# Reordering the end of a block: one tile's norm and transposes earlier, another tile's square later

## The chip, the cores and the metric

One core of one Trainium2 chip runs one launch. The metric is the device time of that launch in microseconds (us). The kernel before was first measured at a median of 326.28 us (326.25 to 327.42, 3 runs).

## The reference, cut to what matters

Linear attention with a cosine weighting, then an RMS norm and a gated feed-forward layer over its output. Only the part from the numerators on is touched by the change.

```python
    num = np.einsum('bhsf,bhfd->bhsd', q_p, kv)
    den = np.einsum('bhsf,bhf->bhs', q_p, z)[..., None] + 1e-06
    return (num / den).astype(np.float32)
    # ... x: 4608 tokens x 512
    rms = np.sqrt(np.mean(x * x, axis=-1, keepdims=True) + 1e-06)
    xn = x / rms * rms_g
    g = xn @ w_gate
    silu = g * (1.0 / (1.0 + np.exp(-g)))
    val = xn @ w_val
    return (silu * val @ w_out).astype(np.float32)
```

## The kernel before

The program order of each engine is fixed by hand. Block 0 is the feed-forward layer of batch 0 (512 tokens). While its last stage, the products with `w_out` ("out products"), runs on TensorE, the attention output of batch 1 is prepared in four tiles of 128 tokens. In this text SBUF is the memory that holds the tiles, PSUM the memory that holds results of TensorE, in banks; the "first out bank" is `banks0[2]`, the one that is copied out first. Each tile goes through the same chain, over all engines:

```python
nd_pe(1, j, psA)      # TensorE: numerators and denominators into PSUM
nd_post(1, j, psA)    # VectorE: rec (L465, L468), division xt = num * rec (L469)
x_sq(1, j)            # ScalarE: square with sum (L480), then an accumulator read;
                      # GpSimd: rs = mean square ^ -0.5, one column (L485, "the power")
x_norm(1, j)          # VectorE: xn = xt * rs * gain row gb, one instruction (L507, "the norm")
x_tr_pe(1, j, bank)   # TensorE: four 128x128 transposes of xn into PSUM (L532)
x_tr_evac(...)        # ScalarE or VectorE: copy of the transposes into xnT
gval_mm(1, n, ...)    # TensorE: gate and value matmuls of block 1, read xnT (L546)
```

The end of block 0 in the kernel before (`out_mm(0, j, n, bank)` is one out product, L566; `tr1` is transposes and a ScalarE copy; `out_store` copies a finished bank out and stores it):

```python
    for n in range(NNT - 2):
        # ... earlier steps cut
        if n == 9:
            tr1(0, psV[0][:, :])
            out_mm(0, 0, n, banks0[0])
        if n in nd_at:                      # n = 4, 6, 8, 9: tiles 0 to 3
            j = nd_at[n]
            nd_pe(1, j, psA)
            nd_post(1, j, psA)
            if n == 9:
                x_norm(1, 1)                # second tile, behind the fourth's division
            x_sq(1, j)
        for j in range(1 if n == 9 else 0, 4):
            out_mm(0, j, n, banks0[j])
    for j in (2, 3):
        for n in (NNT - 2, NNT - 1):
            out_mm(0, j, n, banks0[j])
    out_store(V, 0, 2, banks0[2])
    x_norm(1, 2)
    out_mm(0, 0, NNT - 2, banks0[0])
    tr1(1, psV[1][:, :])                    # second tile's transposes
    out_store(A, 0, 3, banks0[3])
    out_mm(0, 0, NNT - 1, banks0[0])
    # ... two more out products
    gval_mm(1, 0, 0, (0, 256))              # block 1 starts: tiles 0 and 1, step 0
    out_store(A, 0, 1, banks0[1])
    tr1(2, psA[:, 0, :])
    x_norm(1, 3)
    x_tr_pe(1, 3, psC[1][:, :])             # fourth tile's transposes
    x_tr_evac(V, 1, 3, psC[1][:, :])
    gval_mm(1, 1, 1, (0, 256), ((psG, wg),))   # "the gate step" in the text below
```

## Time and profile before

| | kernel before |
|---|---|
| median of the first 3 runs | 326.28 us |
| span of the profiled execution | 323.8 us |
| TensorE busy | 315.8 us, 98% |
| second tile's norm starts / its transposes start | 53.84 / 54.64 us |
| first matmul of block 1 | 55.71 us |
| fourth tile's transposes / gate step | 56.81 / 57.03 us |

TensorE is the bound, so only its waits matter. The prediction shows the lines for them. Two more lines also belong here, from the timelines of VectorE and GpSimd (start us, length us, engine, line, operation, tile written and read):

```profile
55.10 1.41 DVE L507 SCALAR_TENSOR_TENSOR xn<-xt,rs,gb 128x512 bf16<-128x512 f32 x2
```

```profile
54.84 0.55 POOL L485 TENSOR_TENSOR rs<-ms,mhalf 128x1 f32<-128x1 f32 x1 [1.07 <-ACT scr L480]
```

The first is the third and the fourth tile's norm, back to back. The second is the fourth tile's power on GpSimd. It started 0.26 us before the first of these norms and took its usual 0.55 us.

### The profile page before, as it was taken

To read this page: it belongs to the slowest core of one execution; us is meant where nothing else is said; L and a number is where in the kernel's file an instruction comes from. 1 tells how busy PE (TensorE), PEld (TensorE's weight loads), DVE (VectorE), ACT (ScalarE), POOL (GpSimd) and SP (SyncE) were. 2 spreads that over 40 slices of the span, in tenths; PEclk is the share of its full clock that TensorE was granted. 3 is DMA by queue.
4 is the path that set the end of the run, shared out by engine and by line. 5 is a ranking of instruction groups with operands and counts; after the bars stand their busy time and mean duration, and the time that the engine had idled before them with its cause. 6 is when DMAs were issued, how large, how long until landed. Compare 5 with 4: busy or idle time off the path is not lost.

```text
span 323.8 us, 6006 instructions
## 1 busy us (share of the span) xinstructions
PE 315.8 (98%) x2185; PEld 162.4 (50%) x2220; DVE 183.9 (57%) x392; ACT 172.6 (53%) x343; POOL 40.3 (12%) x87
## 2 busy tenths in 40 slices
PE   8899999999999999999999999999999999999995
PEld 3587465654445444544454445444544444444443
DVE  6975677877666765577257745772577133203410
ACT  6974775864765466546564466455644333223321
POOL 4660202101110120012001120120011000000000
PEclk9999999999999999999999999999999999999999
DMA  7999999999699885986596669766721400020014
GB/s 280 284 199 236 300 216 301 263 200 181 171 276 210 222 197 162 179 224 196 162 251 162 179 193 214 195 160 213 107 57 35 130 32 2 29 101 0 2 33 98
DMA packets 93600, 53.88 MB, mean 166 GB/s; under 512 B 58497, under 2 KB 88193, under 8 KB 93570
## 3 DMA queue, kind: packets, MB, share of 16 engines
q1 hardware_dynamic: 86528, 48.65, 60.0%
q0 software_dynamic: 6880, 4.72, 9.8%
q8 instruction: 17, 0.28, 0.4%
q10 hardware_dynamic: 162, 0.13, 0.2%
q14 instruction: 13, 0.11, 0.1%
HBM read 37.75 MB, written 9.44 MB: 146 GB/s over the span
## 4 chain that ended last, share of the span: by engine, by line
PE 93%; DVE 3%; DMA 1%; issue 1%; ACT 1%; DVEq 0%
PE psV L546 27%; PE psG L546 27%; PE psC L566 26%; PE psA L370 3%; PE psA L414 2%; DVE kpm L254 1%; PE psG L566 1%; PE psG L693 1%; DMA rk<-in_k_dram 1%; PE psV L693 1%; PE psO L693 1%; PE psV L321 1%; DVE qp L254 0%; PE psA L422 0%; PE psG L977 0%
## 5 line engine op out<-in xcount | busy, mean ns | idle before, releaser
L561 DVE TENSOR_TENSOR hT<-psV,sg 128x512 bf16<-128x512 f32 x102 | 70.4, 690 | 96.3 <-PE psV L546 72.3
L555 ACT ACTIVATE sg<-psG 128x512 f32<-128x512 f32 x102 | 60.7, 595 | 66.6 <-PE psG L546 65.4
L546 PE MATMUL psV<-xnT,wv 128*128 128x512 bf16 (+1 forms) x365 | 92.1, 374 | 0.4
L546 PE MATMUL psG<-xnT,wg 128*128 128x512 bf16 (+1 forms) x352 | 90.8, 374 | 0.7
L566 PE MATMUL psC<-wo,hT 128*128 128x512 bf16 x382 | 88.5, 379 | 0.7
L546 PEld LDWEIGHTS <-wv 128*128 128x128 bf16 x416 | 40.7, 98 | 47.3
L566 PEld LDWEIGHTS <-hT 128*128 128x128 bf16 x420 | 40.2, 98 | 46.6
L546 PEld LDWEIGHTS <-wg 128*128 128x128 bf16 x416 | 38.7, 98 | 40.5 <-issue 0.3
L485 POOL TENSOR_TENSOR rs<-ms,mhalf 128x1 f32<-128x1 f32 x36 | 19.8, 551 | 182.1 <-ACT scr L480 182.1
L337 ACT COPY osb<-psC 128x512 f32<-128x512 f32 (+1 forms) x33 | 19.1, 580 | 43.0 <-PE psC L566 42.3
L507 DVE SCALAR_TENSOR_TENSOR xn<-xt,rs,gb 128x512 bf16<-128x512 f32 x35 | 26.4, 758 | 16.6 <-POOL rs L485 16.5
L480 ACT ACTIVATE scr<-xt 128x513 bf16<-128x513 f32 x36 | 22.8, 635 | 23.3 <-DVE xt L469 23.2
L252 ACT ACTIVATE kpm<-rk,tab 128x512 bf16<-128x512 f32 (+2 forms) x50 | 26.8, 587 | 1.6 <-DMA rk<-in_k_dram 1.6
L469 DVE TENSOR_TENSOR xt<-psA,rec 128x512 f32<-128x512 f32 x35 | 24.2, 692 | 1.2
L252 ACT ACTIVATE qp<-rq,tab 128x512 bf16<-128x512 f32 (+1 forms) x37 | 23.7, 662 | 0.0
L254 DVE TENSOR_SCALAR kpm<-rk,tab 128x512 bf16<-128x512 f32 (+2 forms) x56 | 19.6, 403 | 2.1 <-DMA rk<-in_k_dram 2.1
L254 DVE TENSOR_SCALAR qp<-rq,tab 128x512 bf16<-128x512 f32 (+1 forms) x37 | 16.0, 448 | 0.0
L414 PEld LDWEIGHTS <-qpT 128*128 128x128 bf16 x248 | 11.6, 98 | 6.8 <-ACT qpT L337 0.2
L414 PE MATMUL psA<-kvzs,qpT 128*128 128x65 bf16 x248 | 12.8, 194 | 0.1
L546 PE MATMUL psG<-xnt_tail,wg 128*128 128x512 bf16 x48 | 12.3, 379 | 0.1
L546 PE MATMUL psV<-xnt_tail,wv 128*128 128x512 bf16 x47 | 12.1, 379 | 0.0
L370 PEld LDWEIGHTS <-kpm 128*128 128x128 bf16 x280 | 9.4, 97 | 1.9 <-ACT vvm L337 0.5
(100 smaller groups left out, 187.7 us busy)
## 6 DMA issues: line engine op xcount, KB each, us to landing
out_dram<-osb SPq DMA_DIRECT2D x28, 256.0 KB, 2.5
rk<-in_k_dram SPq DMA_DIRECT2D x21, 256.0 KB, 3.5
rq<-in_q_dram SPq DMA_DIRECT2D x20, 256.0 KB, 3.1
rv<-in_v_dram SPq DMA_DIRECT2D x16, 256.0 KB, 3.0
rq<-in_q_dram SPq DMA_DIRECT2D x2, 1024.0 KB, 9.2
rv<-in_v_dram SPq DMA_DIRECT2D x4, 512.0 KB, 8.3
out_dram<-osb SPq DMA_DIRECT2D x14, 128.0 KB, 2.4
wo<-in_moe_w_out_dram POOLq DMA_DIRECT2D x4, 384.0 KB, 7.3
```

The source lines that it names most:

```text
L252: nc.scalar.activation(out=out_ap, in_=in_ap, func=AF.Relu, scale=scale)
L254: eng.tensor_scalar(out=out_ap, in0=in_ap, scalar1=scale, scalar2=0.0, op0=ALU.mult, op1=ALU.max)
L370: nc.tensor.matmul(pst[:, h % 2, h // 2 * E : (h // 2 + 1) * E], lhsT=kp_of(b)[:, 8 * c + (h if c < 4 else h % 4), :], rhs=vv_of(b)[:, c, ...
L414: nc.tensor.matmul(o[:, g, i, :], lhsT=qpT[(b, 0)][:, h, j * P : (j + 1) * P], rhs=kvz_of(b, h), start=True, stop=True,)
L469: nc.vector.tensor_tensor(out=xt[:, 0:DM].rearrange("p (b h d) -> p b h d", b=2, d=D), in0=o[:, :, :, 0:D], in1=rec[:, :, :].unsqueeze(3). ...
L480: nc.scalar.activation(out=scr[:, :], in_=xt[:, 0 : DM + 1], func=AF.Square, scale=1.0 / math.sqrt(DM), accum_out=ms[:, :],)
L485: nc.gpsimd.tensor_tensor(out=rs[:, :], in0=ms[:, :], in1=mhalf[:, :], op=ALU.pow)
L507: nc.vector.scalar_tensor_tensor(out=xn[:, :], in0=x_of[(b, j)][:, 0:DM], scalar=rs_of[(b, j)][:, :], in1=gb[:, :], op0=ALU.mult, op1=ALU. ...
L546: nc.tensor.matmul(pst[bank][:, cols[0] : cols[1]], lhsT=w[:, t, n * P : (n + 1) * P], rhs=x[:, t, cols[0] : cols[1]], start=(t == 0), sto ...
L555: nc.scalar.activation(out=sg[:, :], in_=psG[bank][:, :], func=AF.Silu)
L561: nc.vector.tensor_tensor(out=hTs[blk][:, n, :], in0=psV[bank][:, :], in1=sg[:, :], op=ALU.mult)
L566: nc.tensor.matmul(bank, lhsT=hTs[blk][:, n, j * P : (j + 1) * P], rhs=wo[:, n, :], start=(n == 0), stop=(n == NNT - 1),)
```

## The change

The intent is to take away TensorE's wait for the second tile's norm. The norm moves ahead of the fourth tile's division, the transposes move ahead of the last eight out products, and the fourth tile's square goes behind the copy of those transposes.

```diff
         if n == 9:
+            x_norm(1, 1)
             tr1(0, psV[0][:, :])
             out_mm(0, 0, n, banks0[0])
         if n in nd_at:
             j = nd_at[n]
             nd_pe(1, j, psA)
             nd_post(1, j, psA)
-            if n == 9:
-                x_norm(1, 1)
-            x_sq(1, j)
+            if n < 9:
+                x_sq(1, j)
         for j in range(1 if n == 9 else 0, 4):
             out_mm(0, j, n, banks0[j])
+    tr1(1, psV[1][:, :])
+    x_sq(1, 3)
     for j in (2, 3):
         for n in (NNT - 2, NNT - 1):
             out_mm(0, j, n, banks0[j])
     out_store(V, 0, 2, banks0[2])
     x_norm(1, 2)
-    out_mm(0, 0, NNT - 2, banks0[0])
-    tr1(1, psV[1][:, :])
     out_store(A, 0, 3, banks0[3])
-    out_mm(0, 0, NNT - 1, banks0[0])
-    for n in (NNT - 2, NNT - 1):
-        out_mm(0, 1, n, banks0[1])
+    for j in (0, 1):
+        for n in (NNT - 2, NNT - 1):
+            out_mm(0, j, n, banks0[j])
```

## The prediction

> **What bounds the kernel now.** I read the page first: the busy shares, then the shares of the chain that ended last.
>
> ```profile
> PE 315.8 (98%) x2185; PEld 162.4 (50%) x2220; DVE 183.9 (57%) x392; ACT 172.6 (53%) x343; POOL 40.3 (12%) x87
> ...
> PE 93%; DVE 3%; DMA 1%; issue 1%; ACT 1%; DVEq 0%
> ```
>
> TensorE is busy in 98% of a 323.8 us span and makes up 93% of the chain. A change of order that removes no matmul can therefore win only where TensorE waits. The view of waits, asked for TensorE and for its weight loads from 46 us to the end, says where that is. From there on one pair of waits names another engine, and both belong to the same instruction (its weight load and its matmul); I left out the waits put down to issue:
>
> ```profile
> PE psV L532 <- DVE xn L507: 0.2, 1, 0.2
> ...
> PEld L532 <- DVE xn L507: 0.6, 1, 0.6
> ```
>
> L532 is a transpose on TensorE, L507 the norm on VectorE that writes what it transposes. The chain in order of time, 52 to 57 us, shows that place, the end of block 0, where batch 1 is normalised and transposed between the last out products of block 0:
>
> ```profile
> 52.44 0.33 PE psA L414 x8
> ...
> 52.80 0.18 DVE rec L465
> ...
> 53.00 0.21 DVE rec L468
> ...
> 53.23 0.69 DVE xt L469
> 53.93 0.67 DVE xn L507
> 54.60 0.04 issue
> 54.64 0.40 PE psV L532 x4
> 55.04 0.65 PE psC L566 x3
> 55.69 0.03 issue
> 55.71 0.60 PE psG L546 x4
> ```
>
> From 52.8 to 54.6 us the chain runs over VectorE, not TensorE: it divides the fourth tile's numerators (L465 to L469), only then norms the second tile (L507), and TensorE waits for that norm. The timeline of TensorE gives the lost time (start us, length, instruction):
>
> ```profile
> 52.81 1.46 PE L566 MATMUL psG<-wo,hT 128*128 128x512 bf16 x6
> 54.10 0.38 PE L566 MATMUL psC<-wo,hT 128*128 128x512 bf16 x1
> 54.64 0.40 PE L532 MATMUL psV<-ident,xn 128*128 128x128 bf16 x4 [0.16 <-DVE xn L507]
> 54.88 0.81 PE L566 MATMUL psC<-wo,hT 128*128 128x512 bf16 x3
> 55.71 0.60 PE L546 MATMUL psG<-xnT,wg 128*128 128x256 bf16 x4
> ```
>
> Six products start 52.81 to 54.10, so 0.215 us from start to start. The product at 54.10 should be followed at 54.32, but the transposes start at 54.64: **0.32 us lost**. Three products from 54.88 should let the next block's first matmul start at 54.88 + 3 x 0.215 = 55.53; it starts at 55.71: **another 0.18 us**. The timeline of ScalarE explains the second: its copy of the second tile's transposes starts at 55.08 and takes 0.59 us, to 55.67, and the matmul reads that copy. Both losses, 0.50 us, have one cause: the second tile's norm is late. The "[0.16" counts only from the modelled end of the matmul, so I use starts.
>
> **What the Trainium skill says.** "TensorE: Matmul & The Clock Gate", section "Part 2: What happens when you issue a matmul", puts back-to-back 512-column matmuls at about 216 ns; the trace agrees with 0.215 us, so I count in that stride and not in the 0.38 us of one record. The same section says that weight loads may be pulled ahead but matmuls stay in program order. The trace agrees: the out products behind the waiting transposes needed nothing from VectorE and still started only at 54.88. "VectorE: DVE Perf Modes", section "The DRAIN you can't avoid", says the next operation doesn't start until the pipe is empty. Here the norm after the 0.69 us division starts 0.61 us after its start (53.23 to 53.84), so the trace shows a small overlap and I use measured start-to-start distances. "PSUM — Partial Sum Buffer", section "Engine vs sequencer instructions", calls the ScalarE and VectorE queues strict FIFO, which is why moving one instruction in them delays what it is put ahead of.
>
> **The change part by part.** The order of the two builds differs in 30 listed lines on TensorE, 13 on VectorE and 8 on ScalarE; instruction counts are equal. Nothing is removed: four steps move.
>
> 1. Norm of the second tile ahead of the fourth's division. Its input is ready: GpSimd's power ran at 51.24 for 0.55 us, to 51.79. The third tile's division starts at 51.61, so the norm starts at 51.61 + 0.61 = 52.22, against 53.84, and ends after its 0.74 us at 52.96. A weight load followed the old norm by 0.06 us (54.58 to 54.64), so it can start at 53.02. Cost: the fourth tile's first operation starts at 52.22 + 0.66 = 52.88 (the same distance as from 53.84 to the next at 54.50), against 52.80; its division starts at about 53.31 and ends at 54.00 instead of 53.92. It is 0.08 us later because VectorE was waiting 0.49 us there anyway.
>
> 2. Transposes of the second tile ahead of the eight last out products. The last product of step 9 starts at 53.03 (the second of the six above), so the transposes' turn is at 53.24, and their weight loads would naturally go 0.22 us before, at 53.02. The norm is just in time. Four transposes take 0.22 us (51.84 to 52.06 in the first tile's). Eight products follow from 53.46 for 8 x 0.215 = 1.73 us, so the next block's first matmul has its turn at **55.19 instead of 55.71: 0.52 us gained**. Its inputs are ready: transposes end at 53.64, the ScalarE copy runs 53.68 to 54.27. Its bank must be copied out first: its last product ends near 54.06, the copy on VectorE runs from about 54.15 to 54.83. Neither holds it.
>
> 3. The fourth tile's square behind that copy. The ScalarE queue starts it 0.48 us after the copy, at 54.16, against 54.04. The accumulator read follows at 54.70 and ends at 54.89; GpSimd follows by 0.07 us, 54.96 to 55.51. So its scale is 0.12 us later than before (55.39).
>
> 4. The fourth tile's own transposes become the next limit. Before, its norm started at 55.77 behind the third's, and the scale had long been there. Now the third's norm starts near 54.75 and VectorE is free at 55.42, but the scale comes at 55.51; norms follow the power by 0.04 us (80.78 + 0.55 to 81.37 in a later block), so 55.55 to 56.29, weight load at 56.35. TensorE reaches these transposes after eight half-width matmuls (0.87 us, 55.71 to 56.58 before) and the third tile's transposes (0.22 us): 55.19 + 0.87 + 0.22 = 56.28. It waits **some 0.07 us**. The matmuls after them start, with 0.24 us from waiting transpose to next matmul (54.64 to 54.88), at 56.59. Before it was 57.03.
>
> The sum on the path: 0.52 - 0.08 = **0.44 us gained at 57 us**. Downstream the second half of the first step needs the fourth tile's copy, which before ended at 57.72 for a start at 57.90; both move together. After 57 us no wait of TensorE on another engine is listed, so all later work should shift by the same 0.44 us. That is 0.13% of the time: 326.28 - 0.44 = 325.84, which I round to 325.85.
>
> **Rivals.**
>
> (a) The later square takes the place of the wait removed. The fourth tile now depends on transposes, copy, square, read, power, norm in a row: a slip of the second tile's norm by 0.1 us passes to the fourth's transposes as 0.1 us. The weight load of the second tile has 0.00 us to spare at 53.02. With slips of 0.1 to 0.2 us only 0.25 to 0.35 us would be left: about 326.0. For it speaks that the margins are that thin; against it that most distances used are measured on the same instructions 2 us apart.
>
> (b) The full 0.50 to 0.55 us comes through, if the fourth tile's scale arrives earlier than I count: about 325.75. For it: the wait I add is 0.07 us, within the error of my sums.
>
> (c) A transfer sets the next stage and the gain is given back. The value load of batch 2 is late: GpSimd waits for it 5.15 us, until 60.54. Against it: VectorE's casts of that load run at 64.85 and 66.05 behind other work and TensorE's first use of it starts at 66.56, so 4 us stand between. If it were true the time would be unchanged, 326.3.
>
> (d) VectorE becomes the bound and the kernel gets slower, by the norm before the division. VectorE is full from 54 to 56 us (1.00 us busy in each slice of the windows view), so this is its tightest stretch. But it has the same operations and loses an idle 0.49 us; I see at most 0.1 us of loss, 326.4.
>
> **Range and chances.** The steps leave a gain between 0.2 and 0.55 us, so 325.7 to 326.1 by mechanism. The three runs before were 326.25, 326.28 and 327.42, so one run can lie 1.1 us off and the medians may move by a tenth or two; I widen to 325.4 to 326.4. Two per cent would be 6.5 us; the whole stretch touched is 5 us long and held 0.50 us of lost time, so faster by 2% is all but impossible, and slower needs a stall the check of the order doesn't show. Chances: 0.005 faster, 0.985 within, 0.01 slower.
>
> **What would show it right or wrong.** In the changed profile: the norm of the second tile near 52.2 us and its transposes near 53.24, the wait of TensorE on that norm gone or under 0.1 us (step 1 and 2); the next block's first matmul near 55.2 with no idle of 0.18 us before it; the fourth tile's square near 54.16 and its power ending near 55.5 (step 3); the fourth tile's transposes near 56.35 with a small new wait on L507 (step 4); everything after 57 us some 0.44 us earlier, and a span near 323.4. Wrong would be: transposes at 53.4 or later, a first matmul of the next block that still waits for a copy, or a gain at 57 us that is gone by 100 us, which would mean a wait that this trace doesn't show.

## The result, and the profile after

The changed kernel took 326.24 us (median of 6 runs, 325.59 to 327.06). The kernel before, in the same series and its first runs, took 326.77 us (6 runs, 326.25 to 327.78). The ratio is 0.9984 with a 95% interval of 0.996 to 1.0007: the same within 2%, and not distinguishable from no change. A ratio here is the mean time of one kernel's runs over the mean of the other's in the same rounds, so it isn't quite the ratio of the medians quoted.

The profiled execution after has a span of 325.3 us, longer than the 323.8 us of before; it was the slowest of its six (327.06 us). So the two pages must not be subtracted. The busy line and the shares of the chain from its page:

```profile
PE 315.7 (97%) x2185; PEld 162.1 (50%) x2220; DVE 184.0 (57%) x392; ACT 172.6 (53%) x343; POOL 40.6 (12%) x87
...
PE 90%; DMA 4%; ACT 1%; issue 1%; SPq 1%; DVE 1%; POOL 0%; DVEq 0%; POOLq 0%
```

Work is the same, but a transfer and a bit of GpSimd have come into the chain. To compare stages I count from a common origin in both traces: the start of the third tile's division on VectorE (L469), the last instruction ahead of the moved norm. It is at 51.61 us before and 52.04 us after; what lies ahead of it is untouched by the change.

The chain after, in order of time, where before it ran over the fourth tile's division:

```profile
53.84 0.24 PE psV L532 x4
54.07 0.02 issue
54.10 0.40 ACT xnT L337
54.50 0.08 issue
54.58 0.73 ACT scr L480 x2
55.31 0.07 issue
55.38 0.91 POOL rs L485
56.30 0.03 issue
56.32 0.76 DVE xn L507
57.08 0.05 issue
57.13 0.40 PE psC L532 x4
```

The second tile's transposes (L532 at 53.84) no longer wait. The chain now leaves TensorE behind them and runs through copy, square, power and norm of the fourth tile, to its transposes at 57.13. One entry stands out: the power takes 0.9 us. The timelines of VectorE and of GpSimd, the same lines as were shown of before:

```profile
55.14 0.74 DVE L507 SCALAR_TENSOR_TENSOR xn<-xt,rs,gb 128x512 bf16<-128x512 f32 x1
56.32 0.75 DVE L507 SCALAR_TENSOR_TENSOR xn<-xt,rs,gb 128x512 bf16<-128x512 f32 x1 [0.44 <-POOL rs L485]
```

```profile
55.38 0.90 POOL L485 TENSOR_TENSOR rs<-ms,mhalf 128x1 f32<-128x1 f32 x1 [1.19 <-ACT scr L480]
```

The power now starts 0.24 us after the third tile's norm has started, and ends 0.40 us after that norm has ended (55.88 to 56.28). VectorE then sat idle 0.44 us for it. The timeline of TensorE:

```profile
55.62 0.60 PE L546 MATMUL psG<-xnT,wg 128*128 128x256 bf16 x4
56.06 0.60 PE L546 MATMUL psV<-xnT,wv 128*128 128x256 bf16 x4
56.50 0.39 PE L532 MATMUL psA<-ident,xn 128*128 128x128 bf16 x4
57.13 0.40 PE L532 MATMUL psC<-ident,xn 128*128 128x128 bf16 x4 [0.24 <-DVE xn L507]
57.36 0.60 PE L546 MATMUL psG<-xnT,wg 128*128 128x256 bf16 x4
```

| us after the origin | before | predicted | after |
|---|---|---|---|
| second tile's norm starts | 2.23 | 0.61 | 0.61 |
| its transposes start | 3.03 | 1.63 | 1.63 |
| first matmul of block 1 | 4.10 | 3.58 | 3.58 |
| fourth tile's power starts | 3.23 | 3.35 | 3.34 |
| fourth tile's power ends | 3.78 | 3.90 | 4.24 |
| its transposes start | 5.20 | 4.74 | 5.09 |
| gate step | 5.42 | 4.98 | 5.32 |

The change gained 0.52 us at the first matmul of block 1, exactly as worked out, and gave 0.42 us of it back at the fourth tile's transposes. **0.10 us is left at the gate step, not 0.44.**

### The profile page after: what moved, and what is told of

The parts are those of the page before. It is cut to its first block, busy times and chain, and to the rows that moved or that the text cites. A ratio compares the mean times of both kernels' runs of the same rounds, so it can differ in the third digit from the quotient of the medians.

```text
span 325.3 us, 6006 instructions
## 1 busy us (share of the span) xinstructions
PE 315.7 (97%) x2185; PEld 162.1 (50%) x2220; DVE 184.0 (57%) x392; ACT 172.6 (53%) x343; POOL 40.6 (12%) x87
## 4 chain that ended last, share of the span: by engine, by line
PE 90%; DMA 4%; ACT 1%; issue 1%; SPq 1%; DVE 1%; POOL 0%; DVEq 0%; POOLq 0%
PE psV L546 26%; PE psC L566 26%; PE psG L546 25%; DMA rv<-in_v_dram 4%; PE psA L370 3%; PE psA L414 2%; PE psG L566 1%; PE psG L693 1%; PE psV L693 1%; PE psO L693 1%; PE psV L321 1%; PE psA L422 0%; ACT scr L480 0%; SPq L82 0%; PE psG L977 0%
## 5 line engine op out<-in xcount | busy, mean ns | idle before, releaser
L561 DVE TENSOR_TENSOR hT<-psV,sg 128x512 bf16<-128x512 f32 x102 | 70.3, 689 | 97.4 <-PE psV L546 72.8
L469 DVE TENSOR_TENSOR xt<-psA,rec 128x512 f32<-128x512 f32 x35 | 24.2, 691 | 1.2
```

What stands on the lines that cost most here:

```text
L469: nc.vector.tensor_tensor(out=xt[:, 0:DM].rearrange("p (b h d) -> p b h d", b=2, d=D), in0=o[:, :, :, 0:D], in1=rec[:, :, :].unsqueeze(3). ...
L561: nc.vector.tensor_tensor(out=hTs[blk][:, n, :], in0=psV[bank][:, :], in1=sg[:, :], op=ALU.mult)
```

## The experiments

Two theories. **P**: the power on GpSimd stands still while the third tile's norm, an instruction with two inputs in SBUF, runs on VectorE. The Trainium skill states such a rule, in "SBUF — State Buffer", section "Who interferes with whom": "A DVE instruction with two SBUF inputs contends with a GpSimd instruction that reads SBUF". **Q**: the square that was put behind a copy is what makes the fourth tile late. A third question came with the first runs: does what is gained at the gate step reach the end?

### The changed kernel again: after_again

No edit.

> The changed kernel once more. All times below are counted from the start of the third tile's division on VectorE (L469, the last before the moved norm), so that executions whose opening took longer can be compared. Theory P (the fourth tile's power on GpSimd stands still while the third tile's norm, which reads two tiles from SBUF, runs on VectorE): the power takes 0.90 us again, the fourth tile's transposes start 5.09 and the first matmul of the next gate step 5.32 us after the origin, 0.10 us earlier than in the kernel before (5.42); the whole time is then only 0.1 us below before, a ratio near 0.9997. Rival C (the 0.90 us was an accident of that one execution): the power takes 0.55, the two come at 4.72 and 4.95, and the ratio is near 0.9985.

Measured: the power took 0.90 us again, transposes at 5.09, gate step at 5.33. Time 325.97 us (6 runs, 325.47 to 326.57) against 325.83 us (11 runs); ratio 1.000 (0.9981 to 1.002). Theory P's numbers hold to 0.01 us and the long power is no accident. The times of the stage repeat far better than the whole time does.

### Third tile's norm out of the way: third_first

```diff
-    out_store(V, 0, 2, banks0[2])
     x_norm(1, 2)
+    out_store(V, 0, 2, banks0[2])
```

> The third tile's norm is put ahead of the copy of the first out bank on VectorE, so it ends some 0.3 us before the fourth tile's power starts. Theory P: the power takes 0.55 us, the fourth tile's norm starts 3.93 us after the origin, its transposes come at 4.75 and the next gate step at 4.97; the first matmul of the next block waits for the later bank copy and starts at 3.66 instead of 3.58. Rival Q (the moved square is late because it sits behind the copy in the ScalarE queue, and that alone delays the fourth tile): the power ends as late as before, the transposes stay at 5.09 and the gate step at 5.32, or later.

Measured, timeline of GpSimd and of VectorE (the norm that waited is the fourth tile's):

```profile
54.93 0.55 POOL L485 TENSOR_TENSOR rs<-ms,mhalf 128x1 f32<-128x1 f32 x1 [1.19 <-ACT scr L480]
```

```profile
55.51 0.75 DVE L507 SCALAR_TENSOR_TENSOR xn<-xt,rs,gb 128x512 bf16<-128x512 f32 x1 [0.28 <-POOL rs L485]
```

The power starts 3.34 us after the origin, as in the changed kernel, and takes 0.55 us. First matmul of block 1 at 3.70, fourth tile's transposes at 4.80, gate step at 5.03. Theory P was right in the mechanism and 0.06 us off, mostly because the later bank copy held TensorE a little longer (3.70 for 3.66). Q falls: the square is as late as in the changed kernel, and the gate step is 0.29 us earlier. Time 325.75 us (6 runs) against 325.83 us, ratio 1.000 (0.9979 to 1.0022): nothing of it shows in the whole time. This execution had a wait of 0.69 us near 70 us, to which I come back.

### One input moved to PSUM, result wrong on purpose: psum_gain

```diff
     out_store(V, 0, 2, banks0[2])
-    x_norm(1, 2)
+    xn = four.tile([P, DM], BF16, name="xn", tag="xn")
+    nc.vector.scalar_tensor_tensor(
+        out=xn[:, :].rearrange("p (a c) -> p a c", a=2),
+        in0=x_of[(1, 2)][:, 0:DM].rearrange("p (a c) -> p a c", a=2),
+        scalar=rs_of[(1, 2)][:, :],
+        in1=psA[:, 1:2, 0:256].to_broadcast([P, 2, 256]),
+        op0=ALU.mult, op1=ALU.mult,
+    )
+    xn_of[(1, 2)] = xn
```

> Wrong result on purpose: the third tile's norm takes its second tensor from a PSUM bank instead of the gain row in SBUF, in the same place, of the same length, so that it reads one tensor from SBUF only. Theory P: the power, though it still starts while that norm runs, takes 0.55 us, and the fourth tile's transposes come near 4.72 and the gate step near 4.95. Rival Q, or any rival in which the place in time and not the second SBUF input makes the power long: 0.90 us, 5.09 and 5.32 unchanged.

Measured, timeline of VectorE and of GpSimd:

```profile
54.98 0.73 DVE L934 SCALAR_TENSOR_TENSOR xn<-xt,rs,psA 128x512 bf16<-128x512 f32 x1
```

```profile
55.22 0.55 POOL L485 TENSOR_TENSOR rs<-ms,mhalf 128x1 f32<-128x1 f32 x1 [1.19 <-ACT scr L480]
```

This is the sharpest of the tests. The instruction is in the same place and of the same length, the power starts 0.24 us into it as in the changed kernel, and yet it takes 0.55 us. Transposes at 4.73, gate step at 4.97. The second SBUF input was taken away, so that input is what makes the power stand still. (The stand-in also reads the same 256 columns twice; a change of that access pattern alone was not run, but the instruction's length did not move by more than 0.01 us.)

### The same overlap made in the kernel before: before_third_first

The edit is that of third_first, applied to the kernel before.

> The kernel before, with the third tile's norm ahead of the first bank's copy, which puts that norm over the power, where in the kernel before they only touched. Theory P: the norm runs from 2.89 to 3.63, the power starts at 3.23 as before but takes 0.80 us (0.40 after the norm's end) instead of 0.55. Later bank copy: next block at 4.29 instead of 4.10, gate step near 5.62. Rival (the long power belongs to the changed kernel's place): 0.55 us.

Measured: the norm ran from 2.89 to 3.64, the power started at 3.23 and took 0.81 us, to 4.04, again 0.40 us after the norm's end. Block 1 started at 4.29, the gate step came at 5.62. The changed kernel isn't needed for the effect.

### First part alone: norm_alone

```diff
         if n == 9:
+            x_norm(1, 1)
             tr1(0, psV[0][:, :])
...
-            if n == 9:
-                x_norm(1, 1)
             x_sq(1, j)
```

> Only the first part of the change: the second tile's norm ahead of the fourth's division; its transposes and the square stay where they were. Counted from the third tile's division. Theory P (power and two-tile norm exclude each other): the transposes no longer wait and start at 2.71, the copy behind the square ends at 3.74, so the next block starts at 3.78; the first out bank is done earlier than in the full change, so the third tile's norm runs from 2.91 to 3.65, the power starts at 3.30 inside it and ends 0.40 us after it, at 4.05 (0.75 us long); fourth tile's transposes at 4.90, next gate step at 5.13, so this part alone gains 0.29 us on the kernel before, more than the full change's 0.10. Rival (the parts add up, and the full change is the better): next gate step later than 5.32.

Measured, group of the power over the whole kernel (shortest/median/longest in ns), of this kernel and then of the kernel before:

```profile
L485 POOL TENSOR_TENSOR rs<-ms,mhalf x36: 548/550/749, 16.5 to 255.7; 128x1 f32<-128x1 f32 x36
```

```profile
L485 POOL TENSOR_TENSOR rs<-ms,mhalf x36: 548/550/568, 15.4 to 254.1; 128x1 f32<-128x1 f32 x36
```

Of 36 powers one is long, the fourth tile's: from 3.31 to 4.06, behind a norm from 2.91 to 3.65. Transposes at 2.72 without a wait, block 1 at 3.78, fourth tile's transposes at 4.90, gate step at 5.13: every number of the expectation within 0.01 us. So the first part alone gains 0.29 us at the gate step, three times the whole change. The rest of the change takes 0.19 us of that away. It is the earlier transposes that do it, since square_first (next) has them without the later square and comes to the same 5.32: they let the first out bank finish later, so its copy starts at 2.49 instead of 2.31, with it the third tile's norm, and with it the end of the long power. One execution, 327.19 us with a late opening (origin at 52.76 us); its whole time says nothing.

### The square not later: square_first

```diff
-    tr1(1, psV[1][:, :])
     x_sq(1, 3)
+    tr1(1, psV[1][:, :])
```

> The full change without the later square: the fourth tile's square goes ahead of the second tile's transposes and copy again. Theory P: the square starts at 2.51 instead of 2.54, so nothing is won: the power still starts inside the third tile's norm (3.10 to 3.84) and ends at 4.24, the fourth tile's transposes start at 5.09, the gate step at 5.32; the copy comes behind the square and the next block's first matmul starts at 3.62 instead of 3.58. Rival Q (the square put behind the copy is what delays the fourth tile): power ending by 3.9, transposes at 4.75, gate step under 5.0.

Measured: power from 3.30 to 4.24 (0.94 us), fourth tile's transposes at 5.08, gate step at 5.32. Q falls a second time: starting the power 0.04 us earlier only makes it 0.04 us longer. I was wrong on one number: block 1 started at 3.75, not 3.62. I had forgotten that the accumulator read stands between square and copy, so the copy starts at 3.13. The later square does serve the first matmul of block 1, by 0.17 us; the wait at the fourth tile then hides that.

### Second part without the first: transposes_alone

```diff
         if n == 9:
-            x_norm(1, 1)
             tr1(0, psV[0][:, :])
...
             nd_post(1, j, psA)
+            if n == 9:
+                x_norm(1, 1)
```

(against the changed kernel)

> The second part without the first: transposes and square as in the changed kernel, the norm of the second tile behind the fourth's division as before. Matmuls stay in order, so TensorE stands until the norm ends: transposes at 3.03 with nothing before them, next block at 5.0, the power again inside the third tile's norm, fourth tile's transposes near 6.53 and gate step near 6.77: 1.35 us later than in the kernel before.

Measured, timeline of TensorE:

```profile
54.95 0.40 PE L532 MATMUL psV<-ident,xn 128*128 128x128 bf16 x4 [1.23 <-DVE xn L507]
```

Transposes at 3.03 after a wait of 1.23 us, block 1 at 4.99, gate step at 6.73: 1.31 us later than before (1.35 expected). The out products behind the transposes could have run and did not. The earlier transposes are only worth having with the earlier norm.

### A version without the overlap: third_first_value and third_value_again

On top of third_first, block 1 starts with its value half, because its gate bank is now the one copied out last.

```diff
-    gval_mm(1, 0, 0, (0, 256))
+    gval_mm(1, 0, 0, (0, 256), ((psV, wv), (psG, wg)))
```

> As the run before, and the next block's first step takes its value half before its gate half, because the value bank is free early and the gate bank is now the late one. Theory P: first matmul of the next block at 3.58 again, power 0.55 us, fourth tile's transposes at 4.72 and next gate step at 4.95, now bound by the chain of square, power and norm with TensorE waiting under 0.1 us. Rival Q: 5.09 and 5.32 as in the changed kernel. The whole time would be 0.45 us below the kernel before (ratio 0.9986) under P if nothing later takes it back; if the late value load of batch 3, near 97 us, sets the next stage, the whole time moves by less than the gate step does.

> The change with the third tile's norm and the value half first, once more, for the whole time: gate step at 4.97. If the 0.45 us of the stage reach the end in most executions, the ratio is 0.998 to 0.9995 and the fastest execution is some 0.4 us under the fastest of before; if the late value load of batch 3 takes it back, the fastest is still 0.4 us under but the medians are nearly equal.

Measured, both times: power 0.55 us, first matmul of block 1 at 3.59 and 3.58, transposes at 4.74 and 4.73, gate step at 4.97. So this order gains 0.45 us at the gate step, the size that I had predicted for the change itself. The whole time: 325.44 us (6 runs, 325.02 to 327.45) against 325.83 us, ratio 0.9995 (0.997 to 1.0021); the second time 326.19 us (325.48 to 327.41) against 326.34 us, ratio 0.9995 (0.9971 to 1.002). In the first series its fastest execution is 0.5 us under the fastest of before (325.02 to 325.55), in the second 0.1 us (325.48 to 325.58), while its slowest are as slow as those of before. So a fastest execution some 0.4 us under that of before was seen in one series of two.

### Before against itself: before_again

> The kernel before against itself: what a ratio of this kind shows where there is nothing to show. Ratio 1.000 within some 0.002; power 0.55 us long, gate step 5.42 us after the third tile's division. If the waits of TensorE near 97 us (none in the one profile of before) belong to late loads and not to the change, they may show up here too; if the earlier gate step causes them, this profile has none.

Measured: 326.56 us (6 runs, 325.87 to 327.99) against 326.34 us for the same kernel (11 runs), ratio 1.0014 (0.9986 to 1.0043); gate step at 5.41, no wait after it. A difference of the size predicted (0.0013) can't be read from six runs.

### Where the whole time scatters

A table of the profiled executions splits each span at the origin and at the gate step.

| execution | origin at | gate step after origin | gate step to the end | wait after the gate step |
|---|---|---|---|---|
| before | 51.61 | 5.42 | 266.8 | none |
| before_again | 52.18 | 5.41 | 266.8 | none |
| before_third_first | 52.02 | 5.62 | 266.8 | none |
| transposes_alone | 51.92 | 6.73 | 266.8 | none |
| after | 52.04 | 5.32 | 267.9 | near 91 and 97 us |
| after_again | 51.71 | 5.33 | 266.9 | none |
| square_first | 51.76 | 5.32 | 266.8 | none |
| norm_alone | 52.76 | 5.13 | 267.5 | near 70 and 97 us |
| third_first | 51.59 | 5.03 | 267.7 | near 70 us |
| third_first_value | 52.00 | 4.97 | 266.8 | none |
| third_value_again | 51.82 | 4.97 | 268.1 | near 70, 91 and 97 us |
| psum_gain | 51.88 | 4.97 | 267.2 | near 97 us |
| queue_relief | 52.07 | 4.97 | 266.8 | none |
| all_three | 51.79 | 4.97 | 268.3 | near 97 us (0.07 us near 91) |

The opening moves the origin by up to 1.2 us from execution to execution. Where TensorE meets no further wait, 266.8 or 266.9 us follow the gate step, whatever the kernel: then the gain of the stage reaches the end whole. In six executions up to 1.5 us were lost again. Timeline of TensorE in the execution of after, then in that of third_first:

```profile
98.41 0.19 PE L370 MATMUL psA<-vvt,kpm 128*128 128x65 bf16 x1 [0.55 <-POOL vvt L339]
```

```profile
69.94 0.42 PE L414 MATMUL psA<-kvzs,qpT 128*128 128x65 bf16 x8 [0.69 <-DMA qpT<-qp]
```

At 97 us TensorE waits for the cast of batch 3's values, which waits for their load; at 70 us for queries transposed by DMA. Near 91 us the first matmuls of block 2 start up to 0.4 us late, where the waits name a transfer. These transfers are issued from SyncE's queue, in order. In the profile of before the second load of value heads was issued at 89.12 us, in that of after at 91.15 us, though TensorE was only 0.33 us later at the gate step. None of the four executions with a gate step at 5.41 or later had such a wait, six of the ten with an earlier one had (in two of the ten the loads themselves were reordered, as told next). That an earlier TensorE runs into these transfers more often is plausible from that; with so few profiled executions, it isn't shown.

Two runs tried to take the waits away, on top of third_first_value. all_three loads the small last piece of batch 3's values ahead of its second half of heads:

```diff
-                at(b, 14, "post", load_heads, "v", nb, 4, 8)
                 at(b, 14, "post", load_last, "v", nb)
+                at(b, 14, "post", load_heads, "v", nb, 4, 8)
```

> The change, with the third tile's norm first, the value half first, and one thing more: in block 1 the last 64 tokens of batch 3's values are loaded ahead of its last four heads, because in slow executions TensorE waited near 97 us for the cast of just that piece. Theory: gate step at 4.97 as in the run without it; the cast of that piece on GpSimd is done over 1 us ahead of its use, TensorE waits nowhere near 97 us, and the whole time is 0.4 to 0.8 us below the kernel before (ratio 0.9975 to 0.999), with a smaller spread. Rival (the waits near 97 us come from elsewhere, from queue order or transposes by DMA): spread of 1 us or more as before, and a median no better than the run with two of the three, which was 0.4 us below the kernel before.

Measured: 326.46 us (6 runs, 325.15 to 327.33) against 326.63 us (11 runs), ratio 0.9987 (0.9959 to 1.0016). The view of TensorE's waits after 46 us:

```profile
PE psA L370 <- DVE vvm L339: 1.3, 1, 1.3
```

The small piece came in time and the second half of heads, now issued last (at 91.65 us), came 1.3 us late. The expectation failed: reordering the loads moved the wait from one piece to the other.

queue_relief takes a load out of the way instead: the last 64 tokens of batch 3's queries go in behind the values.

```diff
                 n = (0, None, 6)[i] + p if b == 1 else 5 * i + p
+                if (which, nb, p) == ("q", 3, 4):
+                    n = 15
```

> As the run beside it, and the load of the last 64 tokens of batch 3's queries leaves SyncE's queue in block 1 ahead of the value loads and goes in behind them. Theory (SyncE's serial queue sets the value load, so TensorE's waits near 97 us come from what stands in front of it): the last value load of heads is issued 0.5 to 1.3 us earlier relative to the matmuls, TensorE waits nowhere near 97 us, the stretch from the gate step to the end is 266.8 us, and the median is 0.4 us or more below the kernel before. Rival (bandwidth, not the queue, sets it): the load is issued earlier and lands no earlier, with the same scatter.

Measured: 325.53 us (6 runs, 325.20 to 326.72) against 326.34 us (11 runs), ratio 0.9976 (0.9956 to 0.9997), the only interval that lies below 1. third_value_again in the same rounds, without this edit, took 326.19 us. No matmul waits in its profile after the gate step (one weight load waits 0.2 us for transposed queries, which delays no matmul). The second load of heads was issued 32.5 us after the gate step, against 32.9 and 34.2 us in the two executions without the edit, so the issue is earlier, though by less than expected in the first comparison. It beats the kernel before as far as six runs can tell, and barely: one interval of eight that just misses 1 is weak evidence. It wasn't run beside the changed kernel. How much of its 0.8 us belongs to the queue and how much to the gate step stays open.

## Why the prediction was right or wrong

The time lay inside the stated range: 326.24 us, 325.85 predicted, range 325.4 to 326.4. That is not much to be proud of, because the scatter of the executions alone fills this range. By its steps:

**The place of the loss and its cause: right.** TensorE's wait for the second tile's norm is gone.

**Steps 1 and 2: right to 0.01 us.** Norm at 0.61, transposes at 1.63 with no wait, first matmul of block 1 at 3.58 us after the origin. The thin margin of 0.00 us at the weight load held.

**Step 3: right up to the power's start, wrong at its end.** The square stood behind the copy in ScalarE's queue, 0.48 us after its start (54.10 to 54.58), as counted. "GpSimd follows by 0.07 us, 54.96 to 55.51": the power started where I put it (3.34 for 3.35), but took 0.90 us, not the 0.55 us that I took from its earlier records. This term of the sum was mis-sized by 0.35 us. I had written that the third tile's norm would start "near 54.75", thus ahead of the power, in the same section, and didn't ask what the two do to each other. In the profile of before no power had started inside a norm, so all 36 durations there were between 548 and 568 ns: a duration from records holds only for what ran beside them.

That profile did show the effect on another pair, which was overlooked. Timelines of VectorE and of GpSimd in the kernel before, in a later block:

```profile
120.60 0.86 DVE L507 SCALAR_TENSOR_TENSOR xn<-xt,rs,gb 128x512 bf16<-128x512 f32 x1 [2.08 <-POOL rs L485]
```

```profile
120.97 0.75 POOL L339 CAST vvt<-rv 64x256 bf16<-64x256 f32 x1
```

This cast of values on GpSimd starts inside a norm and takes 0.75 us; casts that start inside a product with one SBUF input (L561) take 0.39 to 0.40 us. It happens four times in every one of the 14 profiles. The longest norm of the kernel before (0.86 us, for the usual 0.74) would have led there.

**Step 4: right in kind, wrong in size.** The fourth tile's transposes did become the next limit. "It waits some 0.07 us" became 0.41 us: they were due at 4.68 (the third tile's start at 4.46, and 0.22 us) and started at 5.09. The net gain of the stage was therefore 0.10 us and not 0.44.

**"All later work should shift by the same": right where no transfer comes late**, shown by the constant 266.8 us. In the profiled execution of after it was wrong by 1.1 us, lost near 91 and 97 us, around the value load of batch 3: the prediction's own sign of being wrong, a gain "that is gone by 100 us". In after_again nothing was lost. Rival (c) named a late transfer, but at the values of batch 2 near 60 us, which did no harm; the ones that hurt come later.

**Rivals (a), (b), (d).** (a) had the right chain (transposes, copy, square, read, power, norm in a row) but the wrong cause, a slip of the second tile's norm; square_first shows that the square's place isn't it. (b) did not happen. (d) did not happen: the next block started early.

**A reading of the skill.** The prediction sets the 0.61 us from start to start against "VectorE: DVE Perf Modes", section "The DRAIN you can't avoid", as if the two differed. That section adds that a next operation that isn't held back starts earlier, so the overlap of 0.08 us agrees with it; no sum rests on this.

**The difference in medians.** 0.53 us between the medians looks like the predicted 0.44 us, and isn't evidence for it: the stage gained 0.10 us, the second series of the same kernel showed 325.97 against 325.83 us, and the kernel before against itself 326.56 against 326.34 us. Over the four series the median of the kernel before lay between 325.83 and 326.77 us.

## What to carry to other kernels

Before moving a VectorE instruction with two SBUF inputs, look what GpSimd will start while it runs: here a one-column operation took 0.75 to 0.94 us instead of 0.55, and it hurts where it stands in a chain that TensorE waits for. Look for such a pair elsewhere in the profile first; here it was there, with other instructions. Take a duration from the trace only together with what ran beside it. When a change is worth less than the scatter of whole executions, measure the stage from a common origin in the traces; here that repeated to 0.01 us, while medians of six runs moved by 0.2 us with no change at all.

## What the Trainium skill lacked or had wrong

- "SBUF — State Buffer", section "Who interferes with whom": the rule on two SBUF inputs holds here (0.90 us for 0.55 us, and 0.55 us again with one input in PSUM). The section gives two slow-down factors (6.8 and 1.5) but not when a blocked operation ends. Elsewhere the page has a time for a DMA whose descriptors GpSimd writes (section "A bandwidth-pool intuition that's wrong (but worth ruling out)": the end of the VectorE operation and about 115 ns), none for a GpSimd computation. The runs show that a power blocked by a norm ended 0.40 or 0.41 us after the norm's end in six executions, wherever it had started, and a cast of 64x256 values 0.27 us after it (four times in the kernel before).
- The same section says that issue order decides who blocks, and of the two-port modes that the pair is held for the whole instruction. With GpSimd first, the runs show less than that. A power in the lead did no harm to VectorE: in the kernel before a norm started 0.26 us into it, and both kept their usual 0.74 and 0.55 us; a product with two SBUF inputs (L494) started 0.05 us into another, and took 0.41 us (0.42 us with no power beside it), the power 0.57 us. A cast in the lead did harm: a norm that started 0.08 us into it took 0.86 us for 0.74, 0.12 us more, while the cast still had 0.31 us to run.
- No page that I read says how far a queue that issues transfers in order may fall behind the engines that it feeds: in two executions the same load was issued 32.1 and 33.8 us after the gate step.
